# A gated mix of attention and a Fourier product: the large spectral product written as seven half-size products

## The chip, the cores and the metric

The kernel runs on one core of a Trainium2 chip. The metric is the device time of one execution in microseconds (us), the median of three executions. TensorE (PE) multiplies matrices, VectorE (DVE) and ScalarE (ACT) read its results, GpSimd (POOL) does elementwise work on operands, and SyncE (SP) issues most of the transfers.

## The reference

```python
a = x @ dft_hid_re.T                      # [2048, 512]
b = x @ dft_hid_im.T                      # [2048, 512]
y = dft_seq_re @ a - dft_seq_im @ b       # [2048, 2048] @ [2048, 512], twice
q, k, v = heads(x @ wqkv)                 # 32 heads of 16
o = softmax(q @ k.T / 4) @ v              # 2048 keys, each head
g = sigmoid((x * gate_w).sum(-1))
out = g * (o @ wo) + (1 - g) * y
```

All is float32. The line with `y` is the spectral product that the change rewrites: as one matrix product it is [2048, 4096] @ [4096, 512].

## The kernel before, in words

Products that need more precision than one pass of the reduced format (float32r) gives are split: an operand is copied to a rounded high part, the remainder becomes a low part, and a product is three matmuls (high by high, high by low, low by high).

The array of TensorE is used as two row groups, j = 0 and 1, each with 64 contraction rows. A matmul of one row group writes its own PSUM bank and runs beside one of the other row group. The products of the exponentials with the values (`pv`, L737) use four column groups instead.

Heads are worked in 16 pairs. A step is one block of 128 keys against 1024 queries of one pair, 512 steps in all. It takes four score matmuls (`score`, L725), their exponentials on ScalarE (L707), and a group of `pv` matmuls. Ahead of a pair's scores its row maxima are needed: `scan` (L758) is another score product, whose maximum over 512 keys VectorE takes (L760). Two steps make a macro, `m` in the code.

The execution has four stages, each with an order of the PE's instructions that is written out by hand as tokens: `e0`, `e1` are a score in row group 0 or 1, `c0`, `c1` a scan, `s0`, `s1` a "filling" matmul, most of them of the spectral product (`fill`, L984).

- The front: projections of x, and the first scans.
- 90 macros "singles" (`SINGLES`, `ORDERS`): scores, scans and `pv`, and no filling.
- 72 "blocks" of two macros each (`BLOCKS`, `BLOCK_ORDERS`, `AFTER_HALF`). A block holds 24 `s` tokens of each row group with 16 `e` and up to 16 `c`, or 16 of each row group with 16 `e` and 8 `c`; `pv` matmuls of four steps follow.
- 22 last macros, with the output projection as filling.

In the blocks the spectral product goes row block by row block: 2 phases (real with `a`, imaginary with `b`), 16 row blocks `t`, 16 contraction blocks `s`, 3 matmuls, 2 row groups, each 64 rows by 512 columns (`spectral`). Its coefficients come in units of four contraction blocks: `load_unit` fetches 256 KB through SP, `split_unit` makes `chi` (L253, cast) and `clo` (L254, subtraction) on POOL while PE works on the unit before. The split operands `a` lie in SBUF (`ah`, `al`); those of `b` are made by POOL in the singles (`part_b`), stored and fetched when phase 1 begins (`renew`). When a row block ends, VectorE adds its two banks, `z0` and `z1`, to `y` (`close`, L891 and L893); a next row block may write these banks only after that. In the second phase the half-done `y` is fetched from memory and stored again.

After each half of a pair, `quotients` copies `pvb` out and `divide` scales it: four short transfers on POOL's queue (L776), a reciprocal on VectorE and a transfer (L784), four transfers (L788), and three POOL operations with two stores (L791 to L806), each part some macros later (`staged`).

PSUM in the blocks: five banks shared by scores and scans, `z0` and `z1`, and `pvb`. `Banks` is a table of assumed times by which the code picks one of the five.

## Time and profile before

| what | value |
|---|---|
| median of three executions | 1688.39 us (1688.2 to 1694.67) |
| span of the profiled execution | 1686.6 us |
| PE, DVE, ACT, POOL busy | 99%, 74%, 77%, 42% of the span |
| front; singles; blocks; last macros and end (from the chain and the timeline) | to about 337; to 679.4; to 1555.7; to 1686.6 us |

A busy PE is not PE at its peak, since the ends of its matmuls are modelled. For the stages the starts of instructions say more: from one `pv` group to the next in the chain of waits is one block.

### The profile page before, as it was taken

The numbers are of one execution on the slowest core, as the hardware profiler recorded it, in microseconds if no ns is written. First come the engines' busy times: TensorE is split into PE (matmuls) and PEld (weight loads), VectorE is DVE, ScalarE is ACT, GpSimd is POOL, SyncE is SP. The second block draws the span as 40 slices with busy tenths as digits, with TensorE's granted clock in tenths as the row PEclk, the third lists the DMA queues.
The fourth block names the chain that finished last, engine by engine and source line by source line (L and its number), as shares of the span: only waits on it lengthen the run. The fifth ranks groups of instructions, "written<-read, shape, count | busy, mean of one in ns | idle before, by whom it ended". The sixth has DMA issues, their size and how long they took to land.

```text
span 1686.6 us, 37096 instructions
## 1 busy us (share of the span) xinstructions
PE 1672.5 (99%) x13687; PEld 1070.8 (63%) x13687; DVE 1255.2 (74%) x2356; ACT 1302.3 (77%) x2429; POOL 707.5 (42%) x890
## 2 busy tenths in 40 slices
PE   9999999999999999999999999999999999999997
PEld 7877788833333333767777677666677776666554
DVE  5799899777777777888888888556888888556333
ACT  5689988799999999656666666777656665778885
POOL 1464301454662322454454444444535445445321
PEclk9999999999999999999999999999999999999999
DMA  8664234554542222233332332573332423335512
GB/s 286 232 231 154 69 121 145 177 187 126 144 128 71 63 68 77 64 110 102 92 99 83 101 100 89 150 243 87 118 107 81 128 90 118 104 104 152 160 40 100
DMA packets 140550, 206.62 MB, mean 123 GB/s; under 512 B 58880, under 2 KB 61936, under 8 KB 140368
## 3 DMA queue, kind: packets, MB, share of 16 engines
q1 hardware_dynamic: 97952, 173.49, 33.0%
q0 software_dynamic: 41696, 29.44, 6.6%
q8 instruction: 108, 1.77, 0.4%
q10 hardware_dynamic: 720, 1.31, 0.2%
q14 instruction: 74, 0.61, 0.1%
HBM read 137.89 MB, written 65.81 MB: 121 GB/s over the span
## 4 chain that ended last, share of the span: by engine, by line
PE 96%; issue 1%; ACT 1%; DVE 1%; POOL 0%; DMA 0%; SPq 0%; DVEq 0%; ACTq 0%; POOLq 0%
PE pvb L737 28%; PE z L984 24%; PE s L725 17%; PE s L758 10%; PE xy L371 6%; PE xy L350 6%; PE s L187 5%; PE s L364 0%; PE s L219 0%; POOL xg L561 0%; DMA qs<-q_d 0%; DVE el L468 0%; DVE y L929 0%; ACT eh L467 0%; ACT fold L191 0%
## 5 line engine op out<-in xcount | busy, mean ns | idle before, releaser
L707 ACT ACTIVATE e<-s 128x512 f32<-128x512 f32 (+1 forms) x1862 | 1015.7, 683 | 239.2 <-PE s L758 181.7
L760 DVE TENSOR_REDUCE mx<-s 128x1 f32<-128x512 f32 x1320 | 869.5, 688 | 281.0 <-PE s L758 193.6
L725 PE MATMUL s<-qs,ks 50*128 50x512 f32 x2040 | 621.5, 418 | 0.1
L984 PE MATMUL z<-b,chi 64*128 64x512 f32 x2060 | 510.4, 391 | 0.0
L737 PE MATMUL pvb<-e,va 128*17 128x512 f32 x4096 | 492.7, 595 | 0.0
L725 PEld LDWEIGHTS s<-qs,ks 50*128 50x128 f32 x2040 | 307.6, 185 | 213.5 <-ACT e L707 153.3
L758 PE MATMUL s<-ks,qs 48*128 48x512 f32 x1320 | 423.9, 400 | 0.0
L984 PE MATMUL z<-b,clo 64*128 64x512 f32 x1030 | 336.4, 392 | 0.1
L984 PEld LDWEIGHTS z<-b,chi 64*128 64x128 f32 x2060 | 323.6, 186 | 17.7
L193 DVE CUSTOM_DVE_ANT_0 fold<-s,fold 128x512 f32<-128x512 f32 x364 | 240.1, 689 | 23.9 <-ACT fold L191 7.4
L758 PEld LDWEIGHTS s<-ks,qs 48*128 48x128 f32 x1320 | 223.4, 185 | 35.1 <-issue 20.4
L737 PEld LDWEIGHTS pvb<-e,va 128*17 128x17 f32 x4096 | 92.4, 96 | 241.0 <-issue 234.7
L187 PE MATMUL s<-ks,qs 48*128 48x512 f32 x728 | 230.7, 401 | 1.5 <-ACT fold L191 1.1
L191 ACT ACTIVATE fold<-s 128x512 f32<-128x512 f32 x364 | 201.1, 605 | 27.5 <-PE s L187 26.1
L984 PEld LDWEIGHTS z<-b,clo 64*128 64x128 f32 x1030 | 174.9, 186 | 9.2 <-POOL clo L254 0.9
L254 POOL TENSOR_TENSOR clo<-craw,chi 128x512 fp32r<-128x512 f32 x126 | 162.0, 1286 | 10.4
L253 POOL CAST chi<-craw 128x512 fp32r<-128x512 f32 x126 | 77.3, 614 | 209.9 <-PE z L984 142.3
L776 POOL DMA_DIRECT2D lc<-ob x124 | 62.5, 510 | 243.5 <-ACT ob L772 154.2
L187 PEld LDWEIGHTS s<-ks,qs 48*128 48x128 f32 x728 | 131.7, 184 | 35.5 <-DVE mx L193 11.8
L371 PE MATMUL xy<-w,b 64*128 64x512 f32 x384 | 119.9, 398 | 0.0
L350 PE MATMUL xy<-w,b 64*128 64x512 f32 x384 | 116.5, 391 | 0.0
L929 DVE SCALAR_TENSOR_TENSOR y<-z,g,y 128x512 f32<-128x512 f32 x44 | 32.5, 750 | 74.9 <-PE z L984 73.2
(136 smaller groups left out, 1516.9 us busy)
## 6 DMA issues: line engine op xcount, KB each, us to landing
craw<-cr SPq DMA_DIRECT2D x64, 256.0 KB
craw<-ci SPq DMA_DIRECT2D x64, 256.0 KB
qs<-q_d SPq DMA_DIRECT2D x126, 128.0 KB
ks<-k_d SPq DMA_DIRECT2D x108, 128.0 KB
ab_d<-ab SPq DMA_DIRECT2D x32, 256.0 KB
y_d<-y SPq DMA_DIRECT2D x32, 256.0 KB
b<-bs_d SPq DMA_DIRECT2D x32, 256.0 KB
qs<-q_d SPq DMA_DIRECT2D x126, 64.0 KB
```

The costliest lines, as they stand in the source:

```text
L187: nc.tensor.matmul(ps, rows.q[qb // 8][b:b + 48, qb % 8 * P:(qb % 8 + 1) * P], rows.k[c // 2][b:b + 48, c % 2 * 512:(c % 2 + 1) * 512], st ...
L191: seen_by(nc.scalar.activation(fold[j], ps, AF.Relu))
L193: seen_by(nc.vector.tensor_tensor_reduce(out=fold[j], in0=ps, in1=fold[j], scale=1.0, scalar=-3.0e38, op0=ALU.add, op1=ALU.max, accum_out= ...
L254: sub(lo, raw, hi.bitcast(F32))
L350: ins = nc.tensor.matmul(ps, lhs[64:P], rhs[64:P], start=False, stop=last)
L371: nc.tensor.matmul(ps, lhs[0:64], rhs[0:64], start=n == 0, stop=False)
L707: nc.scalar.activation(e if j is None else e[:, j * 512:j * 512 + 512], ps, AF.Exp, scale=SCALE)
L725: nc.tensor.matmul(ps, rows.k[kb // 8][b:b + 50, kb % 8 * P:(kb % 8 + 1) * P], rows.q[h][b:b + 50, c * 512:c * 512 + 512], start=True, sto ...
L737: nc.tensor.matmul(pvb[r:r + VC, :], va[:, kb, 2 * p + j, :], es[step][c][0][:, j * 512:j * 512 + 512], start=kb == 0, stop=kb == NB - 1, ...
L758: nc.tensor.matmul(ps, rows.q[qb // 8][b:b + 48, qb % 8 * P:(qb % 8 + 1) * P], rows.k[c // 2][b:b + 48, c % 2 * 512:(c % 2 + 1) * 512], st ...
L760: nc.vector.tensor_reduce(mx[p][:, j, qb, c:c + 1], ps, axis=AX.X, op=ALU.max)
L984: nc.tensor.matmul(ps, pr_.lhs(j), pr_.rhs(j), start=group.count[j] == 1, stop=group.count[j] == group.size)
```

## The change

The matrix of coefficients and the operand are each cut in 2 by 2, and the product is made as seven products of halves (`SUMS`: which quarters of coefficients are summed, which quarters of the operand, and to which quarters of `y` the result goes with which sign). Each has 8 row blocks, 16 contraction blocks and 256 columns instead of 512.

- A block is now one row block of one product: 48 `s` tokens of each row group, 256 columns wide, with 16 `e` and up to 16 `c`. There are 56 blocks, and 122 macros of singles instead of 90.
- A unit of coefficients is fetched two blocks ahead. Where a product needs a sum of two quarters, two tiles are fetched and POOL adds them one block ahead (`sum_unit`). The four units of the next block are split at the end of a block: the cast is now on ACT, the subtraction stays on POOL.
- The seven sums of the operand are made in the singles on POOL and stored; a tile `hl[s]` holds high and low part in its halves, and `renew` fetches them one by one while the last row block of a product works.
- `close` adds each of the two banks to one or two halves of `y` (256 columns each), at the end of every block; `y` halves are fetched and stored per product.
- The output projection's operands move to other tiles and are loaded earlier, and its rows (`output_rows`) are loaded in the last block. The last macros keep their orders.

```diff
-SINGLES = 90
-BLOCKS = [24] * 28 + [16] * 12 + [24] * 20 + [16] * 12
+SINGLES = 122
+BLOCKS = 56
+SUMS = (
+    (((1, 1, 1),), (2, 0, -1), ((0, 0, 1), (1, 0, 1))),
+    (((1, 0, 1), (1, 1, -1)), (2, 3, 1), ((0, 0, 1),)),
...
-BLOCK_SCANS = {24: 8, 16: 4}
+BLOCK_SCANS = 8
...
+        def sum_unit():
+            if loaded_:
+                raws, sign = loaded_.pop(0)
+                if len(raws) > 1:
+                    (nc.gpsimd.tensor_add if sign > 0 else nc.gpsimd.tensor_sub)(raws[0], raws[0], raws[1])
+                summed.append(raws[0])
-        def split_unit(copy=nc.gpsimd.tensor_copy, sub=nc.gpsimd.tensor_sub):
-            if raws_c:
...
-                copy(hi, raw)
-                sub(lo, raw, hi.bitcast(F32))
+        def split_unit():
+            if summed:
...
+                nc.scalar.copy(hi, raw)
+                nc.gpsimd.tensor_sub(lo, raw, hi.bitcast(F32))
...
-                    self.rows[j] = self.t + self.slot
+                    self.rows[j] = self.t + (self.slot if kind != "s" or now[0] >= OUTM else self.slot / 2 + 6.0)
...
-                        nc.vector.scalar_tensor_tensor(y, ps, gm[:, t:t + 1], y, op0=ALU.mult, op1=ALU.add)
+                    for row, c, sign, k in to:
+                        by = (gm if sign > 0 else gn)[:, row:row + 1]
+                        if (row, c) not in written:
+                            nc.vector.tensor_scalar_mul(y[:, k], ps, by)
+                            written.add((row, c))
+                        else:
+                            nc.vector.scalar_tensor_tensor(y[:, k], ps, by, y[:, k], op0=ALU.mult, op1=ALU.add)
...
-                        yield Product(group, lambda j, i=i, w=w: state["c"][i // 2][64 * j:64 * j + 64, w, :],
-                                      lambda j, i=i, s=s: (al if i == 1 else ah)[s][64 * j:64 * j + 64, :], enter, leave)
+                        yield Product(group, lambda j, i=i, w=w, s=s: state[s // CS][i // 2][64 * j:64 * j + 64, w, :],
+                                      lambda j, i=i, s=s: hl[s][64 * j:64 * j + 64, HD * (i == 1):HD * (i == 1) + HD],
+                                      enter, leave)
...
+                if m < OUTM - 1:
+                    for _ in range(NU):
+                        split_unit()
-                for _ in range(min(len(late), 1 if closing and m < OUTM - 1 else 5)):
+                for _ in range(min(len(late), 2 if closing and m < OUTM - 1 else 5)):
                     late.pop(0)()
```

First place: PE's queue where a block begins, after the `pv` group (`pvb<-e,va`). `s<-qs,ks` is a score, `s<-ks,qs` a scan, `z<-` the spectral product, with `b` its operand and `chi`, `clo` its coefficients. Before:

```order
L737 MATMUL pvb<-e,va 17x512 x16
L725 MATMUL s<-qs,ks 128x512
L758 MATMUL s<-ks,qs 128x512
L984 MATMUL z<-b_5081,chi 128x512
L725 MATMUL s<-qs,ks 128x512
L984 MATMUL z<-b_5082,chi 128x512
L984 MATMUL z<-b_5081,chi 128x512
L984 MATMUL z<-b_5081,clo 128x512
```

The same place now:

```order
L736 MATMUL pvb<-e,va 17x512 x16
L724 MATMUL s<-qs,ks 128x512
L995 MATMUL z<-b_21016,chi 128x256 x2
L757 MATMUL s<-ks,qs 128x512
L724 MATMUL s<-qs,ks 128x512
L995 MATMUL z<-b_21016,chi 128x256
L995 MATMUL z<-b_21016,clo 128x256
L995 MATMUL z<-b_21016,chi 128x256
```

Two half-width matmuls of the spectral product now stand ahead of the block's first scan, which stood second.

Second place: VectorE's queue around the ends of row blocks, where `mx<-s` is the maximum of a scan and `y<-z` a `close`. Before:

```order
L891 TENSOR_SCALAR y<-z,gm 128x512
L893 SCALAR_TENSOR_TENSOR y<-z,gm,y 128x512
L760 TENSOR_REDUCE mx<-s 128x1 x32
L891 TENSOR_SCALAR y<-z,gm 128x512
L893 SCALAR_TENSOR_TENSOR y<-z,gm,y 128x512
```

Now:

```order
L889 TENSOR_SCALAR y<-z,gm 128x256 x2
L892 SCALAR_TENSOR_TENSOR y<-z,gm,y 128x256 x2
L759 TENSOR_REDUCE mx<-s 128x1 x16
L889 TENSOR_SCALAR y<-z,gm 128x256 x2
L892 SCALAR_TENSOR_TENSOR y<-z,gm,y 128x256 x2
```

Two operations of 512 columns every 32 scans become four of 256 columns every 16 scans.

Third place: POOL's queue over one block of which the scaling of a quotient falls due. `L266` is `sum_unit`, `L276` the subtraction of `split_unit`, and L790 to L805 the scaling:

```order
L276 TENSOR_TENSOR b_17322<-b_17019,b_17321 128x512
L266 TENSOR_TENSOR b_17114<-b_17114,craw 128x512
L266 TENSOR_TENSOR b_17169<-b_17169,craw 128x512
L790 TENSOR_TENSOR ob<-ob,rb 128x512
L797 CAST oh<-ob 128x512
L798 TENSOR_TENSOR ol<-ob,oh 128x512
L805 DMA o_d_0_162<-oh 2x64x512
L805 DMA o_d_1_163<-ol 2x64x512
L266 TENSOR_TENSOR b_17228<-b_17228,craw 128x512
L266 TENSOR_TENSOR b_17285<-b_17285,b_17287 128x512
L276 TENSOR_TENSOR b_17579<-b_17114,b_17578 128x512
L276 TENSOR_TENSOR b_17583<-b_17169,b_17582 128x512
```

Before, about two casts with their subtractions stood between two such parts of a quotient; now it is four additions and four subtractions per block.

More of the change, by code (lines that the diff above doesn't have):

```diff
@@ L854, in output_rest @@
             def output_rest(h):
-                a = [block(24 + 2 * h + i) for i in range(2)]
+                a = [block(12 + 2 * h + i) for i in range(2)]
                 for i in range(2):
@@ L1057, in may_load @@
                 if kind == "y":
-                    return all(t in stored and m > stored[t] + 2 for t in (2 * p, 2 * p + 1))
-                return kind == "scan" or part[0] == "k" or (p + 1) * SCANS <= min(scans) - 16 * bool(late)
+                    return m >= OUTM + 2 * p - 6 and all(t in stored and m > stored[t] + 2 for t in (2 * p, 2 * p + 1))
+                return kind == "scan" or part[0] == "k" or (p + 1) * SCANS <= FRONT or p in shifted
             def prefetch(m):
@@ L1102, in build @@
                     f()
+                if SINGLES - 10 <= m < SINGLES - 2:
+                    load_unit(ap)
                 if m == SINGLES - 1:
-                    for _ in range(3):
-                        load_unit(ap, "craw", 3)
+                    for _ in range(NU):
+                        sum_unit()
+                        split_unit()
+                if OUTM - 14 <= m < OUTM - 2 and m % 2 == 0:
+                    next(operands)
                 if m == SINGLES:
```

227 lines of the change are left out of this document (110 added, 117 removed), and 5 rows, old and new, of the table SUMS.

## Prediction

> **What bounds the kernel now.** First the page's busy times, then the stretches of two stages (columns: length, busy us and instructions of PE, weight load, DVE, ACT, POOL, then clock and DMA).
>
> ```profile
> PE 1672.5 (99%) x13687; PEld 1070.8 (63%) x13687; DVE 1255.2 (74%) x2356; ACT 1302.3 (77%) x2429; POOL 707.5 (42%) x890
> 450.00:500.00 50.00, 50.00 (x372) 18.75 (x370) 35.54 (x58) 50.00 (x80) 36.51 (x54) 1.00 0.53 159
> 676.00:1000.00 324.00, 324.00 (x2753) 231.49 (x2751) 281.71 (x438) 205.23 (x401) 150.77 (x185) 1.00 0.33 95
> ```
>
> In the singles ACT has no idle time at all, so ScalarE's exponentials bound them. A macro has 28 PE matmuls (8 scores, 4 scans, and 16 `pv`, which the trace counts twice per written one), so 372 in 50 us are 13.29 macros: 3.763 us each. In the blocks ACT is busy for 63%, DVE for 87%, and PE sets the pace. How fast, the chain of waits shows by the starts of `pv` groups, and the end of the stage by the first group of 16:
>
> ```profile
> 702.27 3.56 PE pvb L737 x32
> ...
> 965.40 3.56 PE pvb L737 x32
> ...
> 1096.35 3.56 PE pvb L737 x32
> ...
> 1168.57 3.56 PE pvb L737 x32
> ...
> 1555.72 1.84 PE pvb L737 x16
> ```
>
> From 702.27 to 965.40 are 20 blocks of 40 matmuls per row group: 13.157 us each. From 1096.35 to 1168.57 are seven of 28 per row group: 10.317. Twelve matmuls are worth 2.84 us, a slot of 0.2367 us; what remains, 13.157 - 40 x 0.2367 = 3.69, is `pv` and the turn-round. The stage's first matmuls (weight loads, then matmuls):
>
> ```profile
> 679.41 0.18 PEld L725 LDWEIGHTS s<-qs,ks 50*128 50x128 f32 x1 [0.85 <-PE s L758]
> 679.41 0.18 PEld L758 LDWEIGHTS s<-ks,qs 48*128 48x128 f32 x1
> 679.52 0.19 PEld L984 LDWEIGHTS z<-b,chi 64*128 64x128 f32 x1
> 679.52 0.19 PEld L725 LDWEIGHTS s<-qs,ks 50*128 50x128 f32 x1
> ...
> 679.75 0.39 PE L984 MATMUL z<-b,chi 64*128 64x512 f32 x1
> 679.76 0.40 PE L725 MATMUL s<-qs,ks 50*128 50x512 f32 x1
> ```
>
> Two loads begin together, one per row group, and both groups take their next load 0.11 us later: loads of the two groups don't queue behind each other, and a load takes 0.11. The next matmuls follow 0.23 after those loads. A narrow slot can thus be shorter than 0.23, but not than 0.11.
>
> VectorE is close behind PE in a block, as its timeline shows:
>
> ```profile
> 704.15 0.74 DVE L891 TENSOR_SCALAR y<-z,gm 128x512 f32<-128x512 f32 x1
> 704.93 0.75 DVE L893 SCALAR_TENSOR_TENSOR y<-z,gm,y 128x512 f32<-128x512 f32 x1
> 706.33 11.11 DVE L760 TENSOR_REDUCE mx<-s 128x1 f32<-128x512 f32 x16 [0.65 <-PE s L758]
> 719.54 10.78 DVE L760 TENSOR_REDUCE mx<-s 128x1 f32<-128x512 f32 x16 [2.10 <-PE s L758]
> ...
> 731.01 0.75 DVE L893 SCALAR_TENSOR_TENSOR y<-z,gm,y 128x512 f32<-128x512 f32 x1
> 731.67 0.28 DVE L209 TENSOR_REDUCE m<-mx 128x32 f32<-128x128 f32 x1
> ...
> 744.08 0.19 DVE L212 TENSOR_TENSOR clo<-mt,chi 128x32 fp32r<-128x32 f32 x1
> ```
>
> Sixteen scans run without a gap for 10.78 to 11.11 us of 13.157, and a block that ends with two closes leaves VectorE 0.65 idle.
>
> **The change part by part.** Durations are of the profiled execution, span 1686.6, 1.8 under the median.
>
> *Removed.* The 72 blocks, 679.41 to 1555.72: 876.3 us.
>
> *Thirty-two more singles.* 32 x 3.763 = +120.4. PE and DVE have room there; the operand sums of `part_b` are POOL's and nobody in the singles waits for them.
>
> *A narrow slot.* No row shows 256 columns. Half of 0.2367 is 0.118, the low end: nothing would be fixed. The high end comes from what a second pass over 512 columns adds:
>
> ```profile
> L984 PE MATMUL z<-b,chi 64*128 64x512 f32 x2060 | 510.4, 391 | 0.0
> L737 PE MATMUL pvb<-e,va 128*17 128x512 f32 x4096 | 492.7, 595 | 0.0
> ```
>
> A float32 `pv` matmul lasts 595 - 391 = 204 ns longer than a float32r one, I read it as one more pass. Then 0.033 of the slot is fixed, and half the columns cost 0.102 + 0.033 = 0.135. I take 0.125, between them and nearer the low end, since the stage's first slots were 0.23. The Trainium skill, TensorE: Matmul & The Clock Gate, Back-to-back issue gap, gives 262 cycles, 0.109 us, for 256 columns; it also gives 0.216 for 512 where the blocks here show 0.237, so the trace disagrees. By 0.109 PE's part of a block would be 0.77 us less than below.
>
> *A block now.* 16 wide slots and 48 narrow ones per row group: 3.69 + 16 x 0.2367 + 48 x 0.125 = 13.48 us (13.14 at 0.118, 13.96 at 0.135). All 660 scans of a row group that the blocks and singles share are done after 52 blocks (122 x 2 + 52 x 8); the last four lack 8 slots, 11.59 each. The stage: 52 x 13.48 + 4 x 11.59 - 3.56 (the last `pv` lies behind it, as before) = 743.8. PE alone therefore saves 876.3 - 743.8 - 120.4 = 12.1.
>
> *Closes.* 36 of the 52 full blocks feed two halves of `y`, four operations of 256 columns; 16 feed one. By the rows 0.75 at 512 columns and 0.19 at 32, one takes 0.45. Dependent ones start 0.03 after the end of the one before (704.15 to 704.93), an independent one 0.09 ahead of it (731.01 to 731.67): 0.36 to 0.48 each, I take 0.42. The next block's second matmul writes `z1`, so it waits for the last close, and the first scan stands behind it. VectorE's round is 10.95 of scans + 4 x 0.42 + the gap of 0.65 + 0.24 because the first scan is now third in its place (two narrow matmuls ahead) = 13.52, bounds 13.11 to 13.92. Over PE's 13.48: 36 x 0.04 = +1.4. With one target it is 0.84 less and PE rules.
>
> *ACT.* Four casts per block, after the last exponential:
>
> ```profile
> L707 ACT ACTIVATE e<-s 128x512 f32<-128x512 f32 x1684 | 886.9, 637 | 237.9 <-PE s L758 181.7 <-PE s L725 45.3 <-PE z L984 5.2
> L387 ACT CAST b<-raws 128x512 fp32r<-128x512 f32 x16 | 9.6, 621 | 4.4 <-DMA raws<-xT 4.1
> L254 POOL TENSOR_TENSOR clo<-craw,chi 128x512 fp32r<-128x512 f32 x126 | 162.0, 1286 | 10.4
> ```
>
> 2.5 us, in the 3.69 in which no scores arrive: hidden. At the turn from singles to blocks nothing hides the first four: +2.5.
>
> *POOL.* Eight operations of 1.286 are 10.3 of 13.48 us; a quotient's scaling adds 4.96, from the first of these rows to the end of the last:
>
> ```profile
> 723.99 1.29 POOL L791 TENSOR_TENSOR ob<-ob,rb 128x512 f32<-128x512 f32 x1
> ...
> 728.12 0.83 POOL L806 DMA_DIRECT2D o_d<-ol  x1
> ```
>
> 15.25, in one of four blocks, is 1.8 behind. The first `clo` may be late by about 1: after the last score come its matmul (0.4), exponential (0.64), cast (0.62) and subtraction (1.29), 2.95, against 3.69 and some slots until it is read. So 0 to 0.8 in each of ten rounds with additions; I take 0.3: +3.
>
> *DMA.* Coefficients are 12 quarters of 8 x 4 units, 384 transfers instead of 128, 96 MB instead of 32. Over 750 us that adds some 90 GB/s to the 95 above, and 159 ran beside the singles; fetched two blocks, 27 us, ahead: nothing, and if late, the wait falls on POOL's additions. SP's queue can stand behind an addition (a fetch needs its tile), with `y` fetches and `renew` behind it; both have over half a block.
>
> *The end.* `output_rows` is issued half a block, some 6 us, before its first use: 0 to 3, I take +1.
>
> Sum: -12.1 + 1.4 + 2.5 + 3 + 1 = -4.2. Span 1682.4, median 1684.
>
> **The rivals.**
>
> *PE alone rules* (0.22). Slot 0.118, closes overlapped at 0.36, so VectorE's round (13.11 at the fast ends) is under PE's 13.14. The stage is then 52 x 13.14 + 4 x 11.25 - 3.56 = 724.7, with +3.5 for turn and end: 1661. For it speaks that PE set the pace in blocks where VectorE was just as full.
>
> *The closes rule* (0.20), slower than before. Four closes stand between the last scan and the next block's second matmul. From 0.45 us each (round 13.64) the saving is gone. At 0.60, nearer to the 0.75 of the wide one, the round is 14.24, 36 x 0.72 = 26 more than taken: 1710. Against it: half the columns.
>
> *POOL rules* (0.08). It then waits in the middle of its round, as it did for reciprocals:
>
> ```profile
> POOL r_d L784 <- DVE lc L783: 136.6, 26, 8.2
> ```
>
> ```profile
> L776 POOL DMA_DIRECT2D lc<-ob x124 | 62.5, 510 | 243.5 <-ACT ob L772 154.2 <-DVE ob L770 88.9 <-DMA rb<-r_d 0.3
> L788 POOL DMA_DIRECT2D rb<-r_d x124 | 60.7, 498 | 52.0 <-DMA r_d<-lc 51.8 <-issue 0.2
> ```
>
> The wait is 5.25 each. Four blocks of POOL work are 41.2 + 4.96 + 4.0 (four transfers of either row) + about 0.6 (the reciprocal's store) = 50.8, and with the wait 56.0 against 53.9: +2.1 in ten rounds, beside the 3 taken: 1705.
>
> *A narrow slot is no shorter* (0.05). The trace has no stretch with more than one matmul per 0.117 us (2753 in 324). If 0.23 is the floor of a slot, a block is 3.69 + 3.79 + 11.04 = 18.5 and the time about 1962; the change would then not do what it says. The same page of the Trainium skill, What overlaps and what doesn't, has a load overlap running matmuls only where the row group differs; load and stream would then add up. The trace disagrees: the slots of 0.23 would be longer by the 0.11 of a load.
>
> The remaining 0.05 is for transfers or tile reuse that I have not seen.
>
> **How the numbers follow.** My forecast has 0.40, with 1676 to 1693 for the middle halves of slot and closes. Half a per cent, 8.4 us, is about what a measurement can tell. Faster (under 1680): nearly all of 0.22, and a good third of 0.40: 0.37. Slower (over 1696.8): most of 0.20 and 0.08, with the last two cases: 0.28. Same: 0.35. The range leaves out the extreme of the first rival and the fourth, and holds the closes up to 0.60: 1664 to 1712.
>
> **What would show it.** Starts of `pv` groups 13.5 apart (11.6 in the last four); in a row group, narrow matmuls 0.12 to 0.13 apart; VectorE's gap before the first scan under 1 us; POOL's additions without waits for transfers. Wrong: `pv` groups over 13.7 apart, with the second matmul of a block waiting for `y<-z` (closes) or the first `clo` (POOL), or narrow matmuls 0.23 apart.

## The result and the profile after

The changed kernel takes 1853.32 us (median of four executions, 1850.35 to 1867.32) against 1688.3 on the same chip: 1.099 times as long, with a 95% interval of 1.0945 to 1.1028. The forecast was 1684.0 with a range of 1664 to 1712, so it missed by 169 us, ten per cent, in a direction to which it gave 0.28, and by a way that none of its rivals described.

The page shows the profiled execution's busy times, the busiest transfer queue (packets, MB, share of the 16 engines) and the shares of the chain of waits:

```profile
span 1852.1 us, 43645 instructions
...
PE 1731.8 (94%) x15991; PEld 1119.3 (60%) x15991; DVE 1267.7 (68%) x2487; ACT 1447.0 (78%) x2583; POOL 1052.0 (57%) x1230
...
q1 hardware_dynamic: 175136, 290.97, 51.8%
...
PE 53%; DMA 20%; POOL 16%; issue 6%; SPq 3%; DVE 2%; ACT 1%; POOLq 0%; DVEq 0%; ACTq 0%
```

PE was busy for 99% of the span before and is for 94% now. SP's queue, q1, had 33.0% of the transfer engines before. A fifth of the chain is transfers, and 16% is POOL, the engine for which the forecast allowed 3 us.

The starts of `pv` groups in the chain say in which stage the time went:

```profile
842.96 3.56 PE pvb L736 x32
856.29 3.56 PE pvb L736 x32
869.64 3.56 PE pvb L736 x32
...
937.07 3.56 PE pvb L736 x32
962.67 4.51 PE pvb L736 x32
...
1649.57 3.56 PE pvb L736 x32
1662.91 3.56 PE pvb L736 x32
1675.34 3.56 PE pvb L736 x32
...
1722.24 1.84 PE pvb L736 x16
```

The undisturbed blocks are 13.34 us long, the first of the last four 12.43 (1662.91 to 1675.34); 13.48 and 11.59 were forecast. So the block itself is close to what the forecast said. But some take far longer: from 937.07 to 962.67 is one block of 25.60. From 1675.34 to 1722.24 are three of the last blocks, which at 12.4 would take 37.2 us and took 46.9; the very last one alone took 22.1. The blocks from the first group of 32 to the first group of 16 take 1722.24 - 842.96 = 879.3 us. This distance is called "the blocks" below. Before it was 866.6, from 689.10 to 1555.72. The long blocks come in a pattern. With `t` counted from 0 in each product, `t` = 1 to 4 run at 13.3 to 14.8 in most products, while `t` = 5, 6, 7 and `t` = 0 of the next product take 14 to 23 in the middle of the stage (18.8, 16.6, 21.7 and 20.9 in the fourth).

What the engines wait for from 842 to 1600 us, in the waits (total, times, longest):

```profile
DVE y L892 <- DMA y<-y_d: 83.5, 28, 8.2
PE z L995 <- DVE y L892: 48.2, 17, 7.1
PEld z L995 <- DMA b<-bs_d: 31.4, 25, 4.3
PE z L995 <- DMA b<-bs_d: 24.2, 18, 4.1
```

VectorE's `close` waits for the half-done `y`, and PE, whose next row block needs the banks, waits for the `close`. PE also waits for renewed operands (`b<-bs_d`). The forecast had PE wait for a `close` only where VectorE's own work was too long, and it had no wait for `y` or for renewed operands. Two stretches, one in long blocks and one in a quiet block (columns as in the prediction):

```profile
1052.00:1092.00 40.00, 33.18 (x329) 25.37 (x328) 23.50 (x39) 23.21 (x42) 22.55 (x21) 0.86 0.92 263
1120.00:1133.00 13.00, 13.00 (x157) 9.76 (x156) 11.16 (x20) 11.07 (x21) 12.97 (x14) 1.00 0.60 170
```

In the long blocks the transfer engines are 92% busy with 263 GB/s, in the quiet one 60% with 170. The issues of 1052 to 1094 us tell what comes together there, 256 KB each where not said:

```profile
b<-bs_d SPq DMA_DIRECT2D x16, 256.0 KB
b<-cr SPq DMA_DIRECT2D x10, 256.0 KB
craw<-ci SPq DMA_DIRECT2D x6, 256.0 KB
b<-ci SPq DMA_DIRECT2D x5, 256.0 KB
y<-y_d SPq DMA_DIRECT2D x3, 128.0 KB
```

A whole set of 16 operands, coefficients for two and a half blocks, three fetches of `y`, and the rows of the next pair's scores (8 blocks are one pair, as they are one product), all on one queue.

The singles lost time too, which the forecast also had at nothing. Their 244 steps took 491.6 us against 339.7 for 180, about 31 more than 244 undisturbed ones (460.9 in the tenth run below), in four stalls. VectorE at the first one, and the waits of 440 to 820 us:

```profile
469.48 1.29 DVE L759 TENSOR_REDUCE mx<-s 128x1 f32<-128x512 f32 x2 [0.60 <-PE s L757]
475.24 0.25 DVE L782 RECIPROCAL lc<-lc 128x16 f32<-128x16 f32 x1 [4.47 <-DMA lc<-ob]
```

```profile
POOL bsum L1044 <- DMA o_d<-oh: 49.5, 6, 9.0
POOL bsum L1044 <- DMA braw<-ab_d: 41.9, 5, 13.2
...
DVE lc L782 <- DMA lc<-ob: 24.4, 7, 6.2
```

A reciprocal of a quotient stands in VectorE's queue until its row has arrived, with scans behind it. POOL issued that row late (L775 at 471.44, in the chain, between operand sums). POOL itself had been held up: the sum `bsum` of the first operand uses the buffers of `oh` and waits until an earlier `oh` has been stored.

### The profile page after: what moved, and what is told of

It is laid out like the page before. It is cut to its first block, busy times and chain, and to the rows that moved or that the text cites. A ratio compares the mean times of both kernels' runs of the same rounds, so it can differ in the third digit from the quotient of the medians.

```text
span 1852.1 us, 43645 instructions
## 1 busy us (share of the span) xinstructions
PE 1731.8 (94%) x15991; PEld 1119.3 (60%) x15991; DVE 1267.7 (68%) x2487; ACT 1447.0 (78%) x2583; POOL 1052.0 (57%) x1230
## 4 chain that ended last, share of the span: by engine, by line
PE 53%; DMA 20%; POOL 16%; issue 6%; SPq 3%; DVE 2%; ACT 1%; POOLq 0%; DVEq 0%; ACTq 0%
PE z L995 14%; PE pvb L736 12%; PE s L724 8%; PE s L757 5%; PE xy L372 5%; PE s L192 5%; PE xy L393 5%; DMA b<-bs_d 3%; DMA y<-y_d 3%; DMA o_d<-oh 3%; POOL b L1046 3%; DMA craw<-ci 2%; POOL b L266 2%; DMA b<-cr 2%; DMA braw<-ab_d 2%
## 5 line engine op out<-in xcount | busy, mean ns | idle before, releaser
L995 PE MATMUL z<-b,b 64*128 64x256 f32 (+1 forms) x3600 | 418.4, 304 | 45.6 <-DVE y L892 26.3
L757 PE MATMUL s<-ks,qs 48*128 48x512 f32 x1320 | 429.3, 417 | 16.6 <-DVE mx L759 16.4
L995 PEld LDWEIGHTS z<-b,b 64*128 64x128 f32 x3600 | 374.2, 197 | 79.3 <-issue 26.6
L995 PE MATMUL z<-b,chi 64*128 64x256 f32 (+1 forms) x1436 | 220.7, 295 | 33.1 <-DVE y L892 21.8
L276 POOL TENSOR_TENSOR b<-b,b 128x512 fp32r<-128x512 f32 x135 | 170.1, 1280 | 130.5 <-ACT b L275 130.5
L757 PEld LDWEIGHTS s<-ks,qs 48*128 48x128 f32 x1320 | 230.0, 195 | 22.6 <-DVE mx L759 21.9
L995 PEld LDWEIGHTS z<-b,chi 64*128 64x128 f32 x1436 | 193.6, 199 | 40.1 <-issue 20.4
L995 PE MATMUL z<-b,clo 64*128 64x256 f32 x718 | 169.3, 293 | 0.0
L276 POOL TENSOR_TENSOR clo<-b,chi 128x512 fp32r<-128x512 f32 x89 | 112.6, 1280 | 83.3 <-ACT chi L275 83.3
L892 DVE SCALAR_TENSOR_TENSOR y<-z,gm,y 128x256 f32<-128x256 f32 x128 | 57.8, 477 | 119.8 <-DMA y<-y_d 62.5
L266 POOL TENSOR_TENSOR b<-b,craw 128x512 f32<-128x512 f32 x96 | 122.4, 1289 | 14.8 <-PE s L724 6.7
L995 PEld LDWEIGHTS z<-b,clo 64*128 64x128 f32 x718 | 129.1, 198 | 0.9 <-POOL clo L276 0.3
```

Of the source, the lines that this page charges most:

```text
L266: (nc.gpsimd.tensor_add if sign > 0 else nc.gpsimd.tensor_sub)(raws[0], raws[0], raws[1])
L276: nc.gpsimd.tensor_sub(lo, raw, hi.bitcast(F32))
L757: nc.tensor.matmul(ps, rows.q[qb // 8][b:b + 48, qb % 8 * P:(qb % 8 + 1) * P], rows.k[c // 2][b:b + 48, c % 2 * 512:(c % 2 + 1) * 512], st ...
L995: nc.tensor.matmul(ps, pr_.lhs(j), pr_.rhs(j), start=group.count[j] == 1, stop=group.count[j] == group.size)
```

## The experiments

Four theories. A: the order in SP's queue; the `y` fetch is issued in the middle of a block, too late behind other fetches, and every long block follows from it. B: volume; too many bytes come together around the end of a product, and whatever is last in the queue is late. C: round trips of the row maxima at SP's head delay what is queued behind. D, for the singles alone: POOL's queue runs late and holds VectorE. The times, and what the stages took, stand in one table at the end of this section. All runs but two are a single execution, and the four executions of the changed kernel differ by up to 17 us (1850.35 to 1867.32), so a difference of less than that between two times says little by itself; the lengths of stages and the waits in the traces carry the argument.

### One part at a time

**`y` fetched at the start of its block.**

```diff
-                            if s == NB // 2 and i == 0:
+                            if s == 0 and i == 0:
                                 fetch()
```

> The fetch of the half-done y is issued when a block's first product enters instead of in its middle; everything else as in the changed kernel. From its trace: undisturbed blocks take 13.34 us, and the blocks lose 140 us over that, in stalls at whose head VectorE waits for y (83.5 us). Theory A (order): the transfers are late because they stand in one queue, in order, behind others and behind SP's own waits, and y is issued only half a block before its use. Then the loss in the blocks falls by 60 to 110 us: 1745 to 1795. Theory B (volume): the DMA engines can't carry what the blocks ask for at 13.34 us (about 28 MB per product of eight blocks, 265 GB/s), whatever the order. Then the waits move to operands and coefficients and the loss falls by less than 25: over 1828.

1835.12 us; blocks 854.6, 25 shorter. The blocks `t` = 5 and 6 came down to 13.3 to 15.5, but `t` = 7 grew to 23 to 25 in five products, and `t` = 0 of the next product stayed at 21 to 24. Moving the fetch moved most of the loss. A alone fails.

**A tile of its own for the first sum in the singles.**

```diff
-                        raw = lo.bitcast(F32) if n else ap.tile([P, HD], F32, tag="oh", name="bsum")
+                        raw = lo.bitcast(F32) if n else ap.tile([P, D], F32R, tag="craw", name="bsum", bufs=3)[:, 0:HD].bitcast(F32)
```

> In the singles, the first sum of the operand (bsum) is put into a tile of its own ring instead of the one that holds a quotient's high part until its store has landed. The singles of the changed kernel lose 31 to 34 us in four stalls. If POOL's wait for those stores (49.5 us, 6 times) delays the quotients' transfers until a reciprocal blocks VectorE's queue, the four stalls go: 25 to 34 us less, 1820 to 1829. If POOL is late because of its own work or of the fetches of the operand (46.0 us, 6 times), they stay: within 10 us of 1853.

1836.54 us. Of 30.7 us lost in the singles 17.2 were left (478.1 - 460.9), two of four stalls; the expectations from here on count from an undisturbed length some 2.4 us shorter and call these 33 and 20. The result lies between the two cases expected. The tile was one reason for POOL's delay and not the only one.

**No renewals.**

```diff
-                hl[s] = block(s)
-                nc.sync.dma_start(hl[s].bitcast(F32), bs_d[n][s])
+                pass
```

> The operands of the seven products are not fetched anew: all seven use the first one's (96 transfers of 256 KB left out, and the waits for them; five of seven products are made with the wrong operand). It prices the fetches one by one. Theory A: PE's waits for them (55 us) go, and a part of the y waits, since these stand behind them in the queue: 70 to 100 us less, 1753 to 1783. Theory B: 25 of about 170 MB of the stage go, at the 212 GB/s of the slow blocks some 115 us less: 1735 to 1745; the two overlap too far to decide by this run alone.

1796.57 us; blocks 822.2, 57 shorter. That is less than either theory expected, and so decides nothing between them. `t` = 0 of every product became clean (13.3 to 13.4); `t` = 5, 6 and 7 stayed about as they were.

**One quarter of coefficients in place of the sum of two.**

```diff
-                for ph, h, sign in SUMS[n][0]:
+                for ph, h, sign in SUMS[n][0][:1]:
```

> Only the first quarter of coefficients of each product is fetched, and nothing is added: 160 of 384 transfers of 256 KB and all POOL additions are left out (the products are of the wrong coefficients). Theory A: SP no longer stands at fetches that wait for an addition (76 us), but y and the operands are issued where they were: 40 to 90 us less, 1763 to 1813. Theory B: 42 MB less, so the stage would ask for only about 210 GB/s at full pace, what it got: the whole 140 us go, 1710 to 1730.

1765.72 us; blocks 787.5, 92 shorter. By the expectation this is A's range (1763 to 1813), near its fast end, and not B's, by which the whole loss would have gone. `t` = 0 after a change of product is long (19 to 23) and so is the very last block (22.1); the other full blocks run at 13.3 to 14.3. The wait for `y` is nearly gone although its fetch stands where it did:

```profile
DVE y L892 <- DMA y<-y_d: 3.0, 5, 1.3
```

So the `y` fetch in mid-block is in time once there are fewer coefficients around it.

### What stands behind the late `y`

**`y` early, and no renewals** (the edits of the first and third run together).

> Both of the first two edits: y fetched from a block's beginning, and no operand fetched anew (left out as before, so five of seven products have the wrong operand). Alone, the first took 25 us from the blocks and left two blocks of 20 to 25 us at the end of each product; the second cleared these and left three in its middle. Theory A (order): the two burdens are separate waits in one queue, so together they clear nearly all: the blocks lose under 30 instead of 140, 1725 to 1750. Theory B (volume): without the renewals the stage still asks for about 230 GB/s, over the 212 it got, so 40 us or more stay: 1755 or more.

1783.14 us; blocks 804.6. In five products one block, `t` = 7, is still 22 to 25. This is on B's side.

**The `y` fetch on ScalarE's queue.**

```diff
-                            nc.sync.dma_start(y[:, k], y_d[row][:, c * HD:c * HD + HD])
+                            nc.scalar.dma_start(y[:, k], y_d[row][:, c * HD:c * HD + HD])
```

> The fetch of y stays in the middle of a block, but is issued by ScalarE on its own queue instead of SP's. No byte is saved and nothing is earlier by the code. Theory A: y no longer stands behind coefficients, rows and SP's waits, so VectorE's 83 us of waiting for it go and the blocks lose 40 to 100 less: 1755 to 1815. Theory B: all queues share the same engines, so y is as late: over 1835.

1912.78 us, the slowest of all. The waits of 842 to 1600 us:

```profile
PEld s L757 <- ACT e L706: 109.9, 18, 10.3
...
ACT e L706 <- DMA b<-bs_d: 47.0, 4, 12.5
...
DVE y L892 <- DMA y<-y_d: 3.5, 4, 1.6
```

`y` is in time now, 3.5 us, and nothing is gained. The fetch has its own wait, and exponentials stand behind it on ScalarE; PE stands for them. What A asked for was done, and the cost of doing it there was larger than the gain. B was wrong in its reason, too: by it `y` would have been as late as before. The run speaks against this queue for `y`, and decides little between A and B.

**Stores of the operand sums issued by POOL** (with the second run's own tile).

```diff
-                        made.append((step + 3, lambda: nc.sync.dma_start(bs_d[n][s], v.bitcast(F32))))
+                        nc.gpsimd.dma_start(bs_d[n][s], v.bitcast(F32))
```

> The own tile for the first sum (it took the loss of the singles from 33 to 20 us, by two of four stalls), and the stores of the operand's sums issued by POOL when a sum is done instead of by SP three steps later. In the singles SP stood 190 us at these stores, waiting for POOL, and the fetches of the operand for which POOL then waits (52 us) are behind them. If that ring of waits makes POOL late, the last two stalls go too: loss under 6 us, 1818 to 1826. If 96 more transfer instructions on POOL (some 0.55 us each) make it later, the loss stays or grows: 1836 or more.

1837.24 us; the singles lose 24.1 us (485.0 - 460.9) against 17.2 with the tile alone. In this one execution more work for POOL's queue made the singles worse.

**All fetches, no additions.** The products then have only one of the two quarters in them.

```diff
-                if len(raws) > 1:
-                    (nc.gpsimd.tensor_add if sign > 0 else nc.gpsimd.tensor_sub)(raws[0], raws[0], raws[1])
```

> All 384 coefficient transfers, but no additions on POOL (the second quarter is fetched and not used; the products are of the wrong coefficients). Without additions and without the second fetches the blocks lost 48 instead of 140 us. Theory A as SP's waits for POOL's additions: without additions alone most of that goes, 1765 to 1800. Theory B: the bytes are all there, so the loss stays: 1840 or more; between these, both have a share.

1834.72 us; blocks 857.0, 22 shorter. This lies between the two theories, as the expectation allowed. Of the 92 that the second quarters cost, 22 go with the additions (POOL's time, and SP standing at a tile until it is added) and some 70 with the fetches as such (857.0 - 787.5).

### Round trips, bytes, and the best that order can do

**Rows of the next pair loaded three macros after the shift is stored, with `y` early.**

```diff
-                    late.extend(shift(p) + [lambda: shifted.add(p)])
+                    late.extend(shift(p) + [lambda: shifted.update({p: now[0]})])
...
-                return kind == "scan" or part[0] == "k" or (p + 1) * SCANS <= FRONT or p in shifted
+                return kind == "scan" or part[0] == "k" or (p + 1) * SCANS <= FRONT or m >= shifted.get(p, MACROS) + 3
```

> y fetched from a block's beginning, and the loads of a pair's query rows with their maxima held back until three macros after the store of these maxima. The changed kernel issues them as soon as the store is issued, so SP stands at its head until that has landed, and y and coefficients stand behind. With y early and no operands fetched anew, one block of 22 to 25 us was left per product, the one in which this falls. Theory C (round trips: a store and the load that needs it, both in one queue, cost SP the whole backlog of the queue): that block goes to 13.3 to 15, and only the two blocks of the renewals lose, 9 to 10 us per product: the blocks' loss is 50 to 75 us of 140, the time 1765 to 1795. Theory B (volume): the loss goes elsewhere, as from 140 to 115 when y was early: over 1820.

1850.93 us; blocks 865.4, 11 longer than with `y` early alone. The loss moved to where the renewals are: `t` = 7 is at 19 to 23, and the next `t` = 0 went up to 26 to 30 in five of six cases. The waits of 842 to 1600 us:

```profile
PEld z L995 <- DMA b<-bs_d: 50.2, 29, 4.8
DVE y L892 <- DMA y<-y_d: 45.5, 12, 8.4
PE z L995 <- DMA b<-bs_d: 40.8, 24, 4.5
```

C fails: less waiting at `y`, more at renewed operands, no gain.

**The quotient's steps 5, 8 and 11 macros after, not 3, 6 and 9, in the singles, with the own tile.**

```diff
-                    for n, f in zip((3, 6, 9) if m < SINGLES else (3, 5, 7) if p < NP - 1 else (2, 3, 4), divide(*quotients(p, h))):
+                    for n, f in zip((5, 8, 11) if m < SINGLES else (3, 5, 7) if p < NP - 1 else (2, 3, 4), divide(*quotients(p, h))):
```

> The own tile for the first sum, and in the singles the three steps of a quotient 5, 8 and 11 macros after it instead of 3, 6 and 9. The stalls left there begin with VectorE's reciprocal, which waits for a transfer that POOL has issued late, with the scans behind it in VectorE's queue. Two macros are 7.5 us more for POOL. If that lag is all, the singles' loss of 20 us (own tile alone) falls under 5: 1815 to 1822. If POOL falls behind without end, they stay: 1835 or more.

1824.57 us. The singles' 244 steps take 460.9, 30.7 less than in the changed kernel, with no stall left. The stretch from 440 to 790 us, in the changed kernel and in this one:

```profile
440.00:790.00 350.00, 333.41 (x2356) 118.42 (x2352) 225.98 (x370) 320.57 (x505) 235.01 (x377) 0.96 0.44 132
```

```profile
440.00:790.00 350.00, 349.68 (x2582) 128.35 (x2580) 248.16 (x404) 349.73 (x555) 252.96 (x405) 1.00 0.51 147
```

ACT is at 349.73 of 350 again, as in the singles before. This shows D: with the own tile and two macros more for POOL's transfers, VectorE's reciprocal no longer waits. The whole time is 2.6 us above the 1815 to 1822 expected. This run loses some time at the end: the very last block is 12.4 us long, but from the first group of 16 to the end it takes 141.2 against 129.9, and there PE waits for the rows of the output projection (`PE z L995 <- DMA b<-o_d`, 7.0 us).

**The three changes of order together** (`y` early, rows later, quotient later with the own tile).

> The edits of the two runs before this together. The sum of their gains: 1853 less some 65 to 85 in the blocks and 28 to 33 in the singles: 1735 to 1760 by theory C; by theory B over 1790. Faster than the kernel before it is by neither, since the renewals' burst stays.

1810.64 us (1808.31 to 1811.6), 1.0725 times the kernel before (1.0707 to 1.0743). It is the fastest version found that makes the whole product. Blocks 856.5, 23 shorter; but 9.7 of this is the very last block, and the end is 10.1 longer, so that order has given 13 us back in the blocks.

**Half of each renewal.** As the run with rows later, but only the high half of each operand is fetched, 128 KB for 256 KB; the low half stays that of the first product.

```diff
-                hl[s] = block(s)
-                nc.sync.dma_start(hl[s].bitcast(F32), bs_d[n][s])
+                nc.sync.dma_start(hl[s][:, 0:HD].bitcast(F32), bs_d[n][s][:, 0:HD])
```

> As the run with the rows later, but of each renewed operand only the high part is fetched: as many transfers and waits, half the bytes (128 KB instead of 256 KB; the low parts stay those of the first product). In the last block of a product 16 renewals come upon 2.1 MB of coefficients. If their bytes are too many for the two blocks they have (theory B for this place: some 9 MB in 27 us), the loss of the two blocks falls from about 10 us per product to under 4: 25 to 45 us less than the run with the rows later. If it is the number of transfers or their waits at SP's head, it stays within 10 us of that run.

1804.52 us; blocks 818.6, 47 shorter than with whole renewals in the same order. As many fetches, half the bytes: bytes count here, as B says. But the two blocks around a change of product did not fall to under 4 us of loss: `t` = 7 still takes 18 to 21 and `t` = 0 takes 19 to 23, against 13.34. Half the bytes took away a good third of what these two lose, so the bytes of the renewals are not the whole of it.

### Is that the whole loss, and is it the rate as such?

**Neither second quarters nor renewals, clean singles** (the edits of the third, fourth and tenth run together).

> Of the changed kernel, with the quotient's steps later and the sum in its own tile as before, this one leaves out the second quarters (64 MB of coefficient fetches, with the additions) and the 96 renewals together, so its values are not the product's. The loss in the blocks was 139 us in the changed kernel; without the renewals alone 57 of it went, without the second quarters alone 92. If these bytes are the whole loss (theory B), nothing is left: every block at 13.3 to 13.4, the last four 12.4, blocks 740 to 748 from the first group of 32 to the first of 16. With front 337.4, singles 461, turn 10.8, end 123 and the 9.4 around them the span is 1682 to 1690, where the forecast's sum was 1682.4; then the terms on PE, closes and ACT held and the term on transfers alone was wrong. If something else of the new arrangement costs (POOL's four subtractions, the closes, the split one block earlier), blocks stay over 755 and the span over 1697.

1689.94 us (1683.07 to 1692.24), 1.0008 times the kernel before (0.9998 to 1.0019). The profiled execution, span 1683.4, by its chain and by the stretch of its blocks:

```profile
811.26 3.56 PE pvb L736 x32
824.60 3.56 PE pvb L736 x32
...
1495.01 3.60 PE pvb L736 x32
1507.47 3.56 PE pvb L736 x32
...
1525.10 5.94 DMA y<-y_d
...
1532.99 9.73 DMA b<-cr
...
1553.57 1.84 PE pvb L736 x16
```

```profile
840.00:1500.00 660.00, 658.91 (x7876) 504.00 (x7870) 572.59 (x989) 539.96 (x997) 373.10 (x385) 1.00 0.53 150
```

Blocks 742.3, in the 740 to 748 expected, and all but one of them at most 14.7. So these two kinds of bytes and POOL's delay make up the difference between the two kernels: 1852.1 - 1683.4 = 168.7, of which 137.0 in the blocks (879.3 - 742.3), 30.6 in the singles' steps (491.6 - 461.0), and 1.8 between the last single and the first block.

It is not all that transfers cost. From 1507.47 to 1553.57 are three of the last blocks, 46.1 us where three of 12.4 would be 37.2: the very last one takes 21.3, nearly as in the changed kernel. The waits of 1497 to 1546 us:

```profile
ACT b L275 <- DMA b<-cr: 7.3, 1, 7.3
...
PE s L724 <- ACT e L706: 6.0, 1, 6.0
```

ScalarE's cast waits for the last coefficients, exponentials stand behind it in ScalarE's queue, and PE waits for these. In the last product a unit is fetched only one block ahead (`late_` in `spectral`), and not two as the list of the change says. SP issued the last two at 1532.49, after the rows of the next pair (from 1526.01 to 1532.39), and they landed 9.7 us later; in the chain they come behind a fetch of `y`. That the expectation came true in its total is therefore partly luck: from the first group of 32 to the first of 16 are 55 blocks and not 56, which undisturbed are 51 x 13.345 + 4 x 12.41 = 730; the missing block and this stall of 8.9 us nearly make up for each other.

The last block and the end together take 151.2 us here and 150 to 154 in all but one of the versions of the changed kernel, against 12.4 + 129.9 = 142.3 without such a wait. No run took this wait away. An estimate from these rows is 1683.4 - 8.9 = 1674.5 us for the profiled execution, 12.1 under the kernel before. It was not run, and the ten executions of this version spread over 9 us, so whether the change would win by 0.7% is not shown.

**The kernel before with 64 MB more, and with 160 MB more.** With each fetch of coefficients go two, or five, more of 256 KB that nobody waits for, into memory that nobody reads.

```diff
+                if tag == "craw":
+                    for k in range(2):
+                        dummy = dram.tile([P, D], F32, tag="dummy", name="dummy", bufs=8)
+                        nc.sync.dma_start(dummy.rearrange("p (c q) -> p c q", q=P), (cr, ci)[ph][(t + k + 1) % NB, :, u * CS:(u + 1) * CS, :])
```

> The kernel before, and with each of its 128 coefficient fetches two more of the same size (256 KB in rows of 512 bytes) from the coefficients into memory that nobody reads: 64 MB more, as many as the change adds in coefficients, spread evenly over the blocks, on the same queue, with no tile to wait for. 95 GB/s becomes about 170. If the rate as such delays transfers (a limit well under 200), the time rises by over 30 us, as it fell by 92 where the changed kernel was spared these bytes. If it is the heap of coefficients, y and renewals in the same blocks (bursts at 260 GB/s), the even load costs under 10 us: 1686 to 1698.

> As the run before, with five more fetches for each: 160 MB more, evenly spread. 95 GB/s would become some 280 at the old pace, above what the slow blocks of the changed kernel got (260 to 266). If that is the limit of what this pattern of transfers gets, the blocks of 24 slots, where most fetches lie, become longer by 5% or more and coefficients come late: over 1720. If transfers take more than that, and the slow blocks came of the order of waits in the queue, the time stays under 1705.

1694.42 and 1808.01 us, one execution each, against 1688.46. The stage of blocks in the kernel before, then with 64 MB:

```profile
676.00:1540.00 864.00, 863.92 (x7348) 594.20 (x7346) 682.52 (x1059) 580.84 (x1141) 406.04 (x503) 1.00 0.37 110
```

```profile
676.00:1540.00 864.00, 861.23 (x7296) 595.20 (x7298) 681.52 (x1057) 577.70 (x1135) 400.62 (x498) 1.00 0.60 183
```

The extra fetches move 66 MB. That is as much as the second quarters and the renewals together: SP's queue moved 67.1 MB less in the run with neither than in the changed kernel, 42 MB of it second quarters (the 64 MB in that run's expectation is what the change adds in coefficients altogether, and not these). Spread evenly, and with nobody waiting for them, they cost 6 us, nearly all of it in one block of 18.9. In the changed kernel the two kinds cost 137. A rate of 183 GB/s in the stage is therefore not the trouble by itself; the changed kernel had 207 from 842 to 1600 us. With 160 MB:

```profile
676.00:1540.00 864.00, 795.86 (x6428) 546.92 (x6432) 621.06 (x965) 505.98 (x977) 355.14 (x439) 0.94 0.84 259
...
760.00:770.00 10.00, 10.00 (x92) 8.03 (x93) 9.34 (x15) 6.85 (x14) 4.06 (x5) 1.00 0.53 149
770.00:780.00 10.00, 6.23 (x56) 3.93 (x45) 4.70 (x7) 5.24 (x10) 2.05 (x4) 1.00 0.37 126
780.00:790.00 10.00, 6.84 (x44) 5.07 (x45) 4.05 (x7) 4.01 (x7) 1.89 (x2) 0.66 0.89 256
...
790.00:815.00 25.00, 24.96 (x212) 17.64 (x212) 20.88 (x34) 15.28 (x30) 10.07 (x13) 1.00 0.97 297
```

The time went over the 1720 expected for a limit of rate. But for 25 us from 790 the engines move 297 GB/s, 97% busy, and PE loses nothing. The time is lost about once a pair, as near 775, where the engines are only 37% to 53% busy: SP's queue shows the rows of the next pair there (`qs<-q_d`, `qs<-m_d`) and five extra fetches that took it 7.34 us to issue, and the coefficients behind them came late (`POOL chi L257 <- DMA craw<-cr`, 11.9 us in two waits). So the expectation was met in its time and not in its reason. In these 25 us a fully used set of engines did no harm; the reading that fits is that what was needed then had been issued far enough ahead, and that a fetch with little lead is hurt when it stands behind much else in this one queue.

The last column has the very last block, which is part of the blocks, and the time from the first group of 16 to the end:

| run | time, us | singles, 244 steps, us | blocks, us | last block and end, us |
|---|---|---|---|---|
| changed kernel | 1853.32 | 491.6 | 879.3 | 22.1 and 129.9 |
| `y` early | 1835.12 | 491.9 | 854.6 | 18.2 and 133.6 |
| own tile | 1836.54 | 478.1 | 872.7 | 18.7 and 132.1 |
| no renewals | 1796.57 | 491.2 | 822.2 | 21.4 and 129.9 |
| one quarter | 1765.72 | 494.7 | 787.5 | 22.1 and 129.9 |
| `y` early, no renewals | 1783.14 | 494.8 | 804.6 | 21.9 and 129.9 |
| `y` on ScalarE's queue | 1912.78 | 491.7 | 935.4 | 15.6 and 131.9 |
| stores by POOL, own tile | 1837.24 | 485.0 | 868.6 | 20.8 and 129.9 |
| no additions | 1834.72 | 491.0 | 857.0 | 18.8 and 131.9 |
| rows later, `y` early | 1850.93 | 491.4 | 865.4 | 12.4 and 139.1 |
| quotient later, own tile | 1824.57 | 460.9 | 870.9 | 12.4 and 141.2 |
| all three orders | 1810.64 | 460.9 | 856.5 | 12.4 and 140.0 |
| rows later, `y` early, half renewals | 1804.52 | 491.4 | 818.6 | 12.4 and 140.9 |
| neither quarters nor renewals, clean singles | 1689.94 | 461.0 | 742.3 | 21.3 and 129.9 |

## Why the prediction was wrong

The step that failed is *DMA*, with its "nothing"; the clause on `part_b` in the singles is the second. By the prediction's own steps, with the last row of the table for those that the loss covers in the changed kernel:

- *Removed, and thirty-two more singles.* 120.4 was right as work: 461.0 - 339.7 = 121.3 for 64 steps. What failed is the clause "the operand sums of `part_b` are POOL's and nobody in the singles waits for them". They share an in-order queue with the quotient's transfers, for which VectorE waits, for whose scans PE waits: 30.7 us, shown by the run with the own tile and the quotient later.
- *A narrow slot.* 0.125 was taken; the undisturbed block of 13.345 gives (13.345 - 3.69 - 16 x 0.2367) / 48 = 0.122. The block was forecast at 13.48. Of the last four blocks the undisturbed ones came out at 12.4 and not 11.59; why was not followed (some 3 us).
- *Closes.* +1.4 forecast, nothing found. In the run with neither, four closes take 1.65, 0.41 each where 0.42 was taken, and VectorE waits 1.2 to 1.7 us for the first scan of a block: it does not set the pace. Three rows of its timeline:

```profile
842.21 10.13 DVE L759 TENSOR_REDUCE mx<-s 128x1 f32<-128x512 f32 x16 [1.67 <-PE s L724]
...
1496.02 1.65 DVE L892 SCALAR_TENSOR_TENSOR y<-z,gm,y 128x256 f32<-128x256 f32 x4
1497.59 0.28 DVE L214 TENSOR_REDUCE m<-mx 128x32 f32<-128x128 f32 x1
```

- *ACT* at the turn: +2.5 forecast; from the last single to the first `pv` group of 32 is 10.8 against 10.6, so nothing. *The end:* +1 forecast for late output rows. From the first group of 16 to the end it is 129.8 in the run with neither, against 130.9 before; but the loss of about 9 us stands right ahead of it, in the last block. Where the last block was clean, the end took 139 to 141, and PE waited for the output rows for 6 to 7 of it. So the turn from the blocks to the last macros cost about 9 us in one place or the other, where this term had 1.
- *POOL.* +3 forecast. The blocks of the run with neither that are not among the last four exceed 13.345 by 3 in sum; whether POOL is the cause there wasn't followed, and that run has no additions.
- *DMA.* "Nothing" was forecast: this is the step that failed, by 137 us in the blocks, with the stall of the last block not counted. It set a mean, 95 + 90 GB/s, against the 159 seen beside the singles. A mean of that size does little harm where nobody waits for the added bytes, as the evenly loaded kernel before shows (6 us at 183 GB/s). But the change's transfers are not even: the operands of a whole product, 4.2 MB, are renewed at once (in 25 us of the stretch shown), and in the same 42 us come coefficients for two and a half blocks, three `y` and rows of a pair. And the lead of "two blocks" holds for coefficients only, and there not in the last product. For `y` and `renew` the step said "both have over half a block", some 7 us. In the long blocks that isn't enough: VectorE's waits for `y` reach 8.2 us.
- *The sum.* With these two kinds of bytes and POOL's delay taken away the profiled span is 1683.4, where the sum was 1682.4. That they agree is luck: 52 blocks came out 0.135 us shorter each, 7 us in all, and the closes, the turn and the end cost 6 less; the stall of 8.9 us in the last block, 3 us of the last four blocks and 2 of the front and the singles make up for it. The median of that run, 1.0008 times the kernel before, is no change by the bound of the prediction; so the small gain forecast (0.3%) was not measured in any run.
- *The rivals.* None of the four was it. That POOL, the closes or the narrow slot would rule is refuted by the undisturbed blocks of 13.34 us; the sign named for the closes, PE's wait for `y<-z`, did appear (48.2 us), but with VectorE waiting for `y`; PE alone rules in undisturbed blocks, but at 0.122 and not 0.118. The 0.05 left "for transfers or tile reuse that I have not seen" held what happened, both parts of it.

What stays open: how the 137 divides between engines that are full and a queue that is in order. Bytes taken away at the place of the burst help (92, 57, 47 us), and as many bytes spread evenly do little, which speaks for their coming together; but the evenly spread ones were also ones that nobody waited for, and no run spread the changed kernel's own fetches. Whether a second queue for `y` that blocks nobody would be enough wasn't tried; the one on ScalarE blocks the exponentials. How much of the loss is the lower clock after each stall was not separated either. No order that was run comes within 7% of the kernel before. With the two kinds of bytes and POOL's delay gone the time is that of the kernel before, with the stall in the last block still in it; what the change would be worth without any of these is open; the estimate made with that run says 12 us.

## What to carry to other kernels

Cost transfers by the block in which they are issued and by the lead that each has, not by a mean over the stage: this change, worth 12 us on PE by the forecast, lost 169 to bursts of transfers and to a queue. In-order queues tie strangers together: list for each new instruction on POOL or SP what stands behind it and who waits for that, however far from the change. And take the new cost away wholly in one run, early: here it put what could still be won at some 12 us, by an estimate, against the 169 lost. Read such a run block by block, for a total that fits can hold two errors that cancel, as the 742.3 us of blocks did here.

## What the runs showed of the hardware

- A matmul of 256 columns in two alternating row groups, each with its own weight load, takes a slot of 0.122 us, worked out from the undisturbed block, where 512 columns take 0.2367: nearly in proportion. In the run with neither, narrow matmuls of a row group start 0.12 us apart (1513.19, 1513.31, 1513.43, 1513.55). The same working from the last blocks of 12.41 gives 0.142, so something else is in those.
- After PE has stood for some us the granted clock falls. In the kernel with 160 MB it is 1.00 while PE stands (770 to 780 us, 6.23 busy of 10) and 0.66 in the next ten; in the changed kernel the `pv` group after the long block lasts 4.51 and not 3.56. So a stall costs more than its own length. The Trainium skill, TensorE: Matmul & The Clock Gate, Part 1, has the clock go to half after an idle window of about 3.4 us; the rows here agree as far as they go: in the ten us ahead of the 0.66 PE stood for 3.77.
- 297 GB/s was moved at 97% busy in the kernel with 160 MB more, 263 at 92% and 170 at 60% in the changed kernel. The extra fetches of the former came as packets of 1.8 KB (SP's queue has 165.2 MB and 90,720 packets more than before), not in rows of 512 bytes as the expectations of these two runs say. The Trainium skill, DMA: Bandwidth & Descriptors, Specifications, gives about 358 GB/s for what memory gives one core; the trace does not bear it out for short times: in the changed kernel five slices of 1.05 us in a row, from 1080.35, moved 382 to 416 GB/s.
